# One tile for each PSUM bank, and dense products by token half from block 1 on

## The chip, the core and the metric

The kernel runs on one core of a Trainium2 chip. The core's engines run at the same time, each through its own queue in order, and meet only at semaphores: TensorE (PE, matrix products), VectorE (DVE), ScalarE (ACT), GpSimd (POOL), and SyncE (SP), whose queue here issues the DMA transfers. Matrix products land in PSUM, which this kernel uses as 8 banks of 512 float32 columns over 128 partitions. The metric is the time of one execution in microseconds on the device; less is better.

## What is computed

Attention over 4 batches and 8 heads of 576 tokens and width 64, with a threshold on the scores, and behind it two gated networks:

```python
scores = scale * q @ k.T
scores = where(scores >= max(scores) - tau, scores, -1e9)
attn   = exp(scores - max(scores)); attn /= sum(attn) + 1e-9
x  = (attn @ v) as [2304, 512]
xn = x / rms(x) * rms_g                          # first network only
y  = (silu(xn @ w_gate) * (xn @ w_val)) @ w_out  # 512 -> 1536 -> 512
z  = (silu(y @ w_gate2) * (y @ w_val2)) @ w_out2
```

All in float32. The networks' products are taken as three products of a high and a low part, so that one product of 384 columns over 128 rows stands three times in the program.

## The kernel before

The 2304 tokens go in three blocks b = 0, 1, 2 of 768, and a block is cut into two token halves of 384 columns, which is what one bank holds of a product. A network of a block is a list of 18 units: 12 for gate and value (`gate_val`), 6 for the output (`outp`), one weight matrix of 128 x 1024 each. Units 0 to 35 are block 0's two networks, 36 to 53 the first of block 1 (b = 1, m = 0), 54 to 71 its second (b = 1, m = 1), 72 to 107 block 2's. From unit 54 on most gate and value units take seven products of half size in place of eight (`gate_val7`, line 985, results read by lines 993, 995 and 1019). All other network products are line 952, in `dense`.

**Attention.** Block 0's attention stands alone at the start: 28 steps of at most two tiles of 128 queries (`fast`). A step is a product for the scores (line 581), the maximum, exponential and threshold (lines 594 to 597), transposes on PE (lines 620 and 625), copies of them out of PSUM (`EV`, lines 665 on DVE and 667 on ACT), the product with v (line 641), and one more copy into X. Block 1's attention is spread between the products of block 0's networks, and block 2's between those of block 1's first network (`tile_ops`): scores at line 685, maximum 699, exponential 701, threshold 702, sums 708, 709 and 712, scaling 521 to 525, split in two float16 parts 536 to 545, transposes by DMA 550, product with v at 734 and 736, and its copies out 746, 748 and 751.

**Banks.** The eight banks are four tiles of two: PB, PD, PA (`ps0`, `ps1`, `ps2` in the profile) and PQ (`ps3`), whose halves are called PC and PE. In block 0's attention PC takes the transposes of a step's first tile and the product with v, PE those of the second. Block 0's networks write both halves of PB and of PD in turn. In block 1's first network a product of one token half takes PB0, PB1 and PD0 in turn (`single_ps`), scores take PA and PQ in turn, and the product with v takes PD1. From unit 54 on PA and PQ are given back and taken again as four tiles of one bank (`pb0` to `pb3`) for `gate_val7`, with PB0 and PD0 as a third bank of each set; `outp` writes both halves of PB and PD again.

**Order and waits.** The code records operations with names of what they read and write, a bank each (PB0, PB1), and gives each a due time; a list scheduler with a cost for each operation then sets one order for all engines (`Program.order`), and the instructions are issued in it. The semaphore waits are not made from those names. A layer below puts them in while it issues, from what the instructions read and write of a tile.

Of the kernel before, what the change touches and what calls it, by code (L numbers as in the profile page):

```python
# [25 lines left out]
P = 128  # L26
# [14 lines left out]
KC = 510  # L41
# [34 lines left out]
for _b, _phases in enumerate(PHASES):  # L76
# [8 lines left out]
NORM_E = [(0, 0, 0, 1, 1, 0, 0, 1, 2, 1, 1, 1), (1, 1, 1, 1, 0, 2, 0, 1, 2, 1, 1, 1), (1, 0, 2, 1, 0, 0, 0, 1, 1, 0, 2, 0)]  # L85
HI_E = [(1, 2, 1, 1, 0, 0, 0, 1, 2, 0, 1, 1), (2, 1, 0, 1, 0, 1, 0, 0, 1, 2, 2, 0), (1, 0, 2, 1, 0, 1, 0, 0, 1, 0, 1, 0)]
# [3 lines left out]
V_E = {1, 3, 6, 7, 8, 12, 14, 15, 16, 21, 24, 27, 28, 29, 30, 31, 32, 34, 37, 38, 39, 40, 44, 46, 47, 48, 51, 53, 55, 56, 58, 59, 61, 68, 69, 82, 83, 87, 96, 97, 102, 107, 108, 109, 110, 113, 116, 118, 119, 120, 121, 122, 123}  # L90
K_E = {1, 3, 6, 7, 8, 12, 14, 18, 19, 20, 22, 24, 25, 26, 30, 31, 32, 33, 34}
W_E = {1, 2, 3, 6, 8, 11, 12, 13, 14, 16, 17, 18, 19, 21, 25, 27, 29, 30, 31, 33, 35, 36, 37, 38, 42, 44, 45, 46, 47, 48, 49, 51, 53, 54, 55, 56, 59, 60, 62, 64, 68, 69, 73, 74, 75, 76, 77, 83, 84, 92, 93, 95, 101, 107, 108, 110, 111, 113, 114, 117, 120, 121, 122, 125, 131, 133, 137, 138, 139, 141, 143}
H_E = {0, 1, 2, 4, 5, 8, 11, 12, 14, 15, 18, 20, 21, 23, 25, 27, 28, 31, 32, 35, 38, 39, 40, 41, 46, 48, 50, 51, 52, 54, 55, 56, 57, 58, 59, 61, 62, 63, 64, 69, 71, 73, 74, 80, 84, 85, 87, 88, 93, 94, 95}
X_E = {2, 6, 10, 11, 14, 15, 16, 18, 21, 24, 25, 29, 31, 32, 33, 34, 35, 39, 40, 41, 43, 44, 46, 48, 51, 54, 55, 57, 58, 60, 61, 62, 63, 66, 67, 74, 75, 81, 82, 83, 84, 86, 88, 89, 90, 91, 93, 94, 95}
P_E = {0, 1, 2, 3, 4, 6, 7, 8, 10, 12, 14, 15, 17, 18, 19, 21, 23, 25, 28, 29, 30}

Q_E = {7, 15, 23, 31, 39, 47, 55, 63, 66, 68, 79, 86, 95, 102, 111, 119, 120, 121, 124, 127, 128, 131, 132, 135, 138, 140, 142, 143, 147, 148, 149, 150, 151, 155, 156, 158, 159, 161, 168, 170, 173, 175, 178, 179, 181, 183, 186, 189, 190, 191}
S_E = (2, 0, 0)
# [20 lines left out]
GP = (-1.55, 1.55, 1.74, 4.96, 5.71, 5.82, 9.5, 4.12)  # L119
# [138 lines left out]
def body(ctx: ExitStack, tc: tile.TileContext, qkv, tau, w1, rg, w2, outT):  # L258
    nc = tc.nc
    sb = ctx.enter_context(tc.tile_pool(name="sb", bufs=1))  # L260
    ps = ctx.enter_context(tc.tile_pool(name="ps", bufs=1, space=bass.MemoryType.PSUM))
# [20 lines left out]
    single = []  # L282

    def bank(i):

        if not single:
            first.__exit__(None, None, None)
            ps2 = ctx.enter_context(tc.tile_pool(name="single", bufs=1, space=bass.MemoryType.PSUM))
            single.extend(ps2.tile([P, 512], F32, name=f"pb{k}") for k in range(4))
        return single[i][:, :HT]  # L290
# [977 lines left out]
```

## Time and profile before

| | us |
|---|---|
| median of 3 runs | 1200.64 (1198.11 to 1203.42) |
| the profiled execution | 1196.99 |
| its span, first to last instruction | 1195.2 |
| PE busy in the span | 1134.5 (95%) |
| DVE, ACT, POOL busy | 873.3, 715.6, 697.7 |

The profiled execution is 3.65 us, 0.3%, under the median, and 1.8 us of it lie outside the span. The time runs through four stages: block 0's attention to 150 us, block 0's networks with block 1's attention to 480, block 1's first network with block 2's attention to about 760, and the rest, products alone, to the end. A row of waits says which engine and line sat idle, and whose end released it; an idle time is worth something only on the engine that sets the stage's end.

### The profile page before, as it was taken

The page shows a single profiled execution, that of the slowest core. Times are in us where ns is not written, and L with a number is a line of the kernel's source. Part 1 is how long each engine was busy: PE and PEld are TensorE (multiplying, and loading weights), DVE is VectorE, ACT ScalarE, POOL GpSimd, SP SyncE. Part 2 cuts the span into 40 slices and gives each one's busy share as a digit, 9 for nine tenths or more (in the row PEclk, how much of TensorE's full clock was granted, in tenths as well). Part 3 has the DMA queues.
Part 4 walks back from the last instruction along what each step waited for, and adds up shares of the span by engine and source line. Part 5 has one row for each costly group of instructions (what it writes and reads, how often), then busy time and mean ns, then how long its engine had stood idle before and what let it go on. Part 6 is the DMA issues. An engine that isn't in the chain of part 4 may idle for free.

```text
span 1195.2 us, 19467 instructions
## 1 busy us (share of the span) xinstructions
PE 1134.5 (95%) x7110; PEld 1043.6 (87%) x7110; DVE 873.3 (73%) x1605; ACT 715.6 (60%) x1037; POOL 697.7 (58%) x813
## 2 busy tenths in 40 slices
PE   8778899999999999999998999999999999999998
PEld 4445699989988898988887877899999999999998
DVE  6788387888878688787767767695777557884844
ACT  4587579787888887644655455454453543544431
POOL 4366407686777787646686666144634735367750
PEclk8999999999999999999999999999999999999999
DMA  5354219999988888966676866412225132222111
GB/s 168 123 194 166 61 59 274 263 290 279 283 250 248 242 274 204 268 184 147 162 163 178 157 147 143 136 72 89 92 85 167 64 123 74 68 89 88 36 54 53
DMA packets 174433, 185.70 MB, mean 155 GB/s; under 512 B 143873, under 2 KB 147713, under 8 KB 164225
## 3 DMA queue, kind: packets, MB, share of 16 engines
q1 hardware_dynamic: 174048, 184.45, 54.3%
q8 instruction: 56, 0.92, 0.3%
q14 instruction: 41, 0.33, 0.1%
q10 hardware_dynamic: 288, 0.00, 0.0%
HBM read 120.46 MB, written 35.65 MB: 131 GB/s over the span
## 4 chain that ended last, share of the span: by engine, by line
PE 72%; DVE 10%; ACT 8%; DMA 4%; issue 3%; POOL 2%; SPq 0%; DVEq 0%; POOLq 0%; ACTq 0%
PE ps L952 38%; PE pb L985 17%; PE ps L685 3%; PE ps L734 3%; PE ps L641 3%; PE ps L985 3%; PE ps L620 2%; ACT arena L667 2%; DMA arena<-arena 1%; PE ps L736 1%; DMA arena<-in_qkv 1%; DVE arena L702 1%; DMA w<-in_w 1%; PE ps L581 1%; DVE col L699 1%
## 5 line engine op out<-in xcount | busy, mean ns | idle before, releaser
L952 PE MATMUL ps<-XS,w 128*128 128x384 f32 x1872 | 349.3, 340 | 16.6 <-DVE th L1046 4.3
L952 PEld LDWEIGHTS ps<-XS,w 128*128 128x128 f32 x1872 | 322.7, 189 | 29.5 <-DVE th L1046 6.6
L952 PE MATMUL ps<-h,w 128*128 128x384 f32 x1704 | 315.2, 338 | 3.6 <-DVE Y L1129 1.6
L952 PEld LDWEIGHTS ps<-h,w 128*128 128x128 f32 x1704 | 296.7, 188 | 9.0 <-DVE Y L1129 2.2
L985 PE MATMUL pb<-rx,arena 128*128 128x384 f32 x528 | 150.3, 339 | 1.0 <-DVE X L794 1.0
L923 POOL TENSOR_TENSOR arena<-w,arena 128x384 fp32r<-128x384 f32 (+1 forms) x84 | 110.3, 1337 | 64.0 <-ACT arena L921 63.5
L985 PEld LDWEIGHTS pb<-rx,arena 128*128 128x128 f32 x528 | 96.7, 188 | 1.2 <-issue 1.2
L702 DVE SCALAR_TENSOR_TENSOR arena<-ps,col,arena 128x576 f32<-128x576 f32 x96 | 77.6, 811 | 25.3 <-ACT arena L701 24.8
L1087 POOL TENSOR_TENSOR h<-th,h 128x768 fp32r<-128x768 f32 (+1 forms) x39 | 61.2, 1574 | 59.2 <-ACT h L1083 59.1
L701 ACT ACTIVATE arena<-ps,col 128x576 f32<-128x576 f32 x96 | 70.6, 738 | 37.5 <-DVE col L700 20.0
L1083 ACT CAST h<-th 128x768 fp32r<-128x768 f32 x72 | 60.1, 835 | 53.3 <-DVE th L1019 38.5
L699 DVE TENSOR_REDUCE col<-ps 128x1 f32<-128x576 f32 x96 | 71.4, 751 | 25.8 <-PE ps L685 25.3
L544 POOL TENSOR_TENSOR arena<-arena 128x512 f16<-128x512 f32 x68 | 86.0, 1268 | 0.2
L985 PE MATMUL pb<-XS,arena 128*128 128x384 f32 x396 | 78.9, 335 | 0.0
L685 PE MATMUL ps<-rx 128*128 128x288 f32 x416 | 71.2, 299 | 3.7 <-DVE arena L702 3.6
L685 PEld LDWEIGHTS ps<-rx 128*128 128x128 f32 x416 | 62.1, 188 | 9.1 <-DVE arena L702 5.4
L985 PEld LDWEIGHTS pb<-XS,arena 128*128 128x128 f32 x396 | 70.0, 188 | 0.0
L921 ACT CAST arena<-w 128x768 fp32r<-128x768 f32 x66 | 61.2, 941 | 14.3 <-DVE w L918 8.2
L856 ACT CAST w<-w 128x1024 fp32r<-128x1024 f32 x49 | 51.4, 1048 | 29.7 <-PE ps L952 18.7
L858 POOL TENSOR_TENSOR w<-w,w 128x1024 fp32r<-128x1024 f32 x23 | 56.6, 2462 | 20.1 <-ACT w L856 20.0
L985 PE MATMUL pb<-ra,arena 128*128 128x384 f32 x198 | 66.9, 338 | 0.0
L918 DVE TENSOR_TENSOR w<-w 128x256 f32<-128x256 f32 x80 | 53.6, 691 | 15.4 <-DMA w<-kept 14.9
(181 smaller groups left out, 2156.5 us busy)
## 6 DMA issues: line engine op xcount, KB each, us to landing
w<-in_w SPq DMA_DIRECT2D x36, 1024.0 KB, 6.3
w<-kept SPq DMA_DIRECT2D x26, 1024.0 KB, 5.4
w<-kept SPq DMA_DIRECT2D x46, 512.0 KB, 3.7
kept<-w SPq DMA_DIRECT2D x17, 1024.0 KB, 5.4
kept<-w SPq DMA_DIRECT2D x25, 512.0 KB, 3.5
arena<-in_qkv SPq DMA_DIRECT2D x40, 160.0 KB, 3.6
ra<-in_qkv SPq DMA_DIRECT2D x10, 576.0 KB, 4.4
out<-Y SPq DMA_DIRECT2D x11, 384.0 KB, 4.6
```

Of the source, the lines that this page charges most:

```text
L544: op(en, 601 if eng == 2 else 1128, lambda: n1.tensor_tensor(h[:, 640:], e[:, :512], h[:, :512], ALU.subtract), lock=True, w=[("lo", n)], ...
L685: nc.tensor.matmul(s[:, j, :HS], x[:, c:c + P], x[:, k:k + HS], start=i + u == 0, stop=i == 1 and u == len(heads) - 1)
L699: op("DVE", 670, lambda: nc.vector.tensor_reduce(c[:, 0:1], s2, AX.XY, ALU.max, negate=True), w=[*sk, ("mx", n)], bufs=[cb], p=T + F['MAX' ...
L701: op("ACT", 640, lambda: nc.scalar.activation(e2, s2, AF.Exp, bias=c[:, 2:3], scale=SCALE), r=[("thr", n)], w=[*sk, ("e", n)] + ek, bufs=[ ...
L702: op("DVE", 750, lambda: nc.vector.scalar_tensor_tensor(e2, s2, c[:, 1:2], e2, ALU.is_ge, ALU.mult, accum_out=c[:, 6:7]), r=[("thr", n)], ...
L858: op(en, 1142 if en == "DVE" else 2340, lambda: n1.tensor_tensor(ws[:, 1], w, f32(ws[:, 0]), ALU.subtract), lock=True, r=[("w32", n), ("wh ...
L921: op("ACT", 939 - 206 * late, lambda a=a, z=z: nc.scalar.copy(sbf.t()[:, 0, a:z], st[:, a:z]), r=[("w32", n)], w=[("wh", n, late)], bufs=[ ...
L923: op(en, 70 + (z - a) * 105 // 100 if en == "DVE" else 190 + (z - a) * 210 // 100, lambda a=a, z=z: n2.tensor_tensor(sbf.t()[:, 1, a:z], s ...
L952: nc.tensor.matmul(pt[:, j, :HT] if len(halves) == 2 else pt, w(i, a), x(i, b_)[:, j * HT:(j + 1) * HT], start=(i == 0 and a == 0 and b_ = ...
L985: nc.tensor.matmul(bank(), w()[:, a, col * 256 + i * P:][:, :P], xf(i, b_), start=first and i == 0 and a == 0 and b_ == 0, stop=i == 1 and ...
L1083: op("ACT", 734, lambda: nc.scalar.copy(h[:, 0], tb.t), r=[("th", n)], w=[("h0", n)], bufs=[tb, hb], p=p + O(n)['HH'], name=f"h{n}")
L1087: op(eng, 72 + (z - a) * 105 // 100 if eng == "DVE" else 190 + (z - a) * 209 // 100, lambda a=a, z=z: n1.tensor_tensor(h[:, 1, a:z], tb.t[ ...
```

## The change

Every bank that is used alone becomes a tile of its own, and the tiles change between stages. At the start PC and PE are two tiles (`pt0`, `pt1`); PA, PB, PD are pairs (`ps0`, `ps1`, `ps2`). Before block 1's networks (`phase` 1) PD becomes PD0 and PD1 (`pbPD0`, `pbPD1`); products of one half take PC, PE and PD0 in turn, scores PA and PB, the product with v PD1. Before unit 54 (`phase` 2) PA and PB become four tiles. Dense products go by token half in all of blocks 1 and 2, so also in the plain units and in `outp` after unit 54, whose results are read 384 columns at a time. The sums of block 2's attention (lines 708 and 709) move from DVE to POOL (`S_E`), and tables and due times are other numbers, of which two lines stand here.

```diff
-S_E = (2, 0, 0)
+S_E = (0, 0, 0)
-UP, UP1, FP, T0, ATT, ATT2, LEAD, LEAD2, END2, UL, RMS0, RMS1, RMS2, CREL = 10544, 14740, 1362, 179133, 22274, -4036, 8, 7.0, 4.0, 13618, -50718, -149645, -594509, 80130
+UP, UP1, FP, T0, ATT, ATT2, LEAD, LEAD2, END2, UL, RMS0, RMS1, RMS2, CREL = 10544, 9643, 1362, 179133, 22274, -69668, 8, 7.5, 8.0, 15712, -50718, -149645, -320154, 80130
...
-    PB, PD = [ps.tile([P, 2, 512], F32, name=f"ps{i}") for i in range(2)]
-    PA = ps1.tile([P, 2, 512], F32, name="ps2")
-    PQ = ps1.tile([P, 2, 512], F32, name="ps3")
-    PC, PE = PQ[:, 0], PQ[:, 1]
+    PC, PE = [open_["C"].tile([P, 512], F32, name=f"pt{i}") for i in range(2)]
+    PA, PB, PD = [open_[k].tile([P, 2, 512], F32, name=f"ps{i}") for i, k in enumerate("ABD")]
+    def bank(key):
+        if key not in ones_:
+            keys = ["PD0", "PD1"] if key in ("PD0", "PD1") else ["PA0", "PA1", "PB0", "PB1"]
+            for k in "D" if key in keys[:2] and len(keys) == 2 else "BA":
+                pools[k].__exit__(None, None, None)
...
+            for k in keys:
+                ones_[k] = p.tile([P, 512], F32, name=f"pb{k}")
+        return ones_[key]
...
-    THREE = [(PB[:, 0, :HT], "PB0"), (PB[:, 1, :HT], "PB1"), (PD[:, 0, :HT], "PD0")]
...
-    def single_ps():
-        third[0] += 1
-        return THREE[third[0] % 3]
+    def single_ps(late_=True):
+        third[0] += 1
+        if phase[0] == 1:
+            key = ("PC", "PE", "PD0")[third[0] % 3]
+        else:
+            key = (("PB0", "PB1") if late_ else ("PC", "PE")) + ("PD0", "PD1")
+            key = key[third[0] % 4]
+        return (lambda: bank(key)[:, :HT]), key
...
-        s, sk = (PQ, ["PC", "PE"]) if n >= 2 * NTB and n % 2 else (PA, BK["PA"])
+        s, sk = (PB, BK["PB"]) if n >= 2 * NTB and n % 2 else (PA, BK["PA"])
...
-        pv_, vk = (PD[:, 1], "PD1") if b == 2 else ((PC, "PC"), (PE, "PE"))[pvt[0]]
+        vk = "PD1" if phase[0] else ("PC", "PE")[pvt[0]]
...
+    SETS = [[(lambda k=k: bank(k)[:, :HT], k) for k in x] for x in (("PC", "PE", "PD0"), ("PA0", "PA1", "PB0"))]
...
-                if b == 1 and m == 0:
+                if b:
...
-                    if b == 1 and m == 0:
+                    if b:
```

Up to about 484 us of the trace every engine has the same instructions in the same order in both programs, which was found by comparing the two orders with line and tile names set aside; what differs there is the tiles and the waits. The first place is DVE in block 0's attention, where L665 (L679 in the change) copies transposes or a step's result out of a bank; a name in brackets is the counter of the engine waited for. Before:

```order
L665 COPY X_83<-ps3_71 128x128 [waits Activation_49]
L594 TENSOR_REDUCE col_106<-ps0_65 128x1 [waits PE_49]
L594 TENSOR_REDUCE col_106<-ps2_70 128x1 [waits PE_49]
L597 SCALAR_TENSOR_TENSOR arena_87,col_106<-ps0_65,col_106,arena_87 128x576 [waits Activation_49,Pool_49]
L597 SCALAR_TENSOR_TENSOR Y_85,col_106<-ps1_66,col_106,Y_85 128x576 [waits PE_49,Activation_49]
L665 COPY X_83<-ps3_71 128x128 [waits Activation_49]
```

The change:

```order
L679 COPY X_90<-pt0_74 128x128 [waits PE_49]
L608 TENSOR_REDUCE col_113<-ps1_77 128x1 [waits PE_49]
L608 TENSOR_REDUCE col_113<-ps0_76 128x1 [waits PE_49]
L611 SCALAR_TENSOR_TENSOR arena_94,col_113<-ps1_77,col_113,arena_94 128x576 [waits Activation_49,Pool_49]
L611 SCALAR_TENSOR_TENSOR Y_92,col_113<-ps2_78,col_113,Y_92 128x576 [waits PE_49,Activation_49]
L679 COPY X_90<-pt0_74 128x128 [waits PE_49]
```

Both copies out of PC into X waited for a copy of ACT, which reads the other bank of `ps3`; now they wait for PE alone.

The second place is PE in block 1's first network, a gate and value unit: L952 (L967) is the dense product, `ps0` is PB, `ps1` is PD, whose other bank takes the product with v. Before, the rows that stand at 640 us of the trace:

```order
L952 MATMUL ps0_65<-XS_84,w2_105 128x384 [waits DVE_49]
L952 MATMUL ps0_65<-XS_84,w2_105 128x384 x5
L952 MATMUL ps1_66<-XS_84,w2_105 128x384 [waits Activation_49]
L952 MATMUL ps1_66<-XS_84,w2_105 128x384 x5
L952 MATMUL ps1_66<-XS_84,w2_105 128x384 [waits Activation_49]
L952 MATMUL ps1_66<-XS_84,w2_105 128x384 x5
L952 MATMUL ps0_65<-XS_84,w2_105 128x384 [waits DVE_49]
L952 MATMUL ps0_65<-XS_84,w2_105 128x384 x11
```

The change, a unit of the same kind:

```order
L967 MATMUL pt0_74<-XS_91,w2_112 128x384 x6
L967 MATMUL pt1_75<-XS_91,w2_112 128x384 x6
L699 MATMUL ps1_77<-rx2_1229 128x288 [waits DVE_49]
L699 MATMUL ps1_77<-rx2_1229 128x288 x3
L967 MATMUL pt1_75<-XS_91,w2_112 128x384 x6
L967 MATMUL pbPD0_4993<-XS_91,w2_112 128x384 x12
L967 MATMUL pt0_74<-XS_91,w2_112 128x384 [waits DVE_49]
L967 MATMUL pt0_74<-XS_91,w2_112 128x384 x11
```

Before, all four runs of products begin with a wait, for a reader of the bank beside; now three tiles turn, and the wait that is left on a dense product stands where a bank comes round again.

The third place is PE in `outp` of block 1's second network, one output of 128 rows and 24 products. Before:

```order
L952 MATMUL ps1_66<-h0_91,w2_105 128x384 [waits DMAHW0_49,Activation_49]
L952 MATMUL ps1_66<-h0_91,w2_105 128x384 x5
L952 MATMUL ps1_66<-h1_92,w2_105 128x384 x6
L952 MATMUL ps1_66<-h2_93,w2_105 128x384 x6
L952 MATMUL ps1_66<-h3_94,w2_105 128x384 x6
L952 MATMUL ps0_65<-h0_91,w2_105 128x384 [waits Activation_49]
L952 MATMUL ps0_65<-h0_91,w2_105 128x384 x5
```

The change:

```order
L967 MATMUL pbPB1_7371<-h0_98,w2_112 128x384 [waits DMAHW0_49,Activation_49]
L967 MATMUL pbPB1_7371<-h0_98,w2_112 128x384 x2
L967 MATMUL pbPB1_7371<-h1_99,w2_112 128x384 x3
L967 MATMUL pbPB1_7371<-h2_100,w2_112 128x384 x3
L967 MATMUL pbPB1_7371<-h3_101,w2_112 128x384 x3
L967 MATMUL pbPD0_4993<-h0_98,w2_112 128x384 [waits Activation_49]
L967 MATMUL pbPD0_4993<-h0_98,w2_112 128x384 x2
L967 MATMUL pbPD0_4993<-h1_99,w2_112 128x384 x3
L967 MATMUL pbPD0_4993<-h2_100,w2_112 128x384 x3
L967 MATMUL pbPD0_4993<-h3_101,w2_112 128x384 x3
```

The same products no longer alternate between the halves of a pair: one half goes through all four h tiles into one bank, then the other half into the next.

## Rows read from the trace of the kernel before

**Rows 1.** busy time by stage; the first row names the columns

```profile
core 0: us, PE busy (x) PEld busy (x) DVE busy (x) ACT busy (x) POOL busy (x), PEclk, DMA share, GB/s
0.00:150.00 150.00, 119.10 (x1072) 79.42 (x1072) 101.14 (x228) 96.49 (x177) 76.33 (x170) 0.95 0.44 142
150.00:480.00 330.00, 324.64 (x1928) 303.43 (x1927) 268.84 (x448) 277.45 (x337) 225.38 (x262) 0.99 0.86 243
480.00:800.00 320.00, 299.04 (x1879) 269.55 (x1878) 246.73 (x596) 170.77 (x276) 193.62 (x211) 1.00 0.66 161
800.00:1150.00 350.00, 350.00 (x2001) 349.83 (x2000) 235.30 (x305) 159.56 (x231) 192.83 (x163) 1.00 0.26 89
```

**Rows 2.** waits of PE, 480 to 800 us: total us, times, longest

```profile
PE ps L952 <- DVE th L1046: 4.3, 7, 0.8
PE ps L952 <- DVE th L1049: 3.2, 3, 1.7
PE ps L952 <- ACT th L1048: 3.0, 4, 0.9
PE ps L952 <- ACT X L748: 2.7, 5, 1.0
PE ps L952 <- DVE Y L1129: 1.6, 2, 1.0
PE ps L952 <- ACT tq L746: 1.5, 3, 0.8
PE ps L952 <- ACT Y L1127: 1.1, 1, 1.1
```

**Rows 3.** timeline of PE, 636 to 646 us, idle before and releaser in brackets

```profile
640.11 1.31 PE L952 MATMUL ps<-XS,w 128*128 128x384 f32 x6 [1.74 <-DVE th L1049]
642.26 1.31 PE L952 MATMUL ps<-XS,w 128*128 128x384 f32 x6 [0.84 <-ACT tq L746]
```

**Rows 4.** waits of PE, 0 to 150 us

```profile
PE ps L620 <- ACT arena L667: 4.9, 10, 1.2
```

**Rows 5.** waits of DVE, 0 to 150 us

```profile
DVE X L665 <- ACT arena L667: 3.9, 5, 1.3
DVE arena L665 <- ACT arena L667: 2.7, 5, 0.9
```

**Rows 6.** timeline, 91 to 95 us: one step of the first attention

```profile
91.28 0.66 PE L620 MATMUL ps<-ident,Y 128*128 128x128 f32 x4
...
91.97 0.27 ACT L667 COPY X<-ps 128x128 f32<-128x128 f32 x1
92.13 0.59 ACT L667 COPY arena<-ps 128x512 f32<-128x512 f32 x1
...
92.78 0.66 PE L620 MATMUL ps<-ident,arena 128*128 128x128 f32 x4 [0.84 <-ACT arena L667]
...
93.65 0.69 DVE L665 COPY arena<-ps 128x512 f32<-128x512 f32 x1 [0.89 <-PE ps L625]
...
94.69 0.33 PE L641 MATMUL ps<-arena 128*64 128x128 f32 x2 [0.46 <-ACT arena L667]
```

**Rows 7.** busy time in a 20 us stretch of block 0's attention

```profile
70.00:90.00 20.00, 15.52 (x155) 9.71 (x155) 17.82 (x41) 18.63 (x29) 13.86 (x22) 1.00 0.66 214
```

**Rows 8.** groups of POOL, whole span: busy us, mean ns, idle before

```profile
L708 POOL TENSOR_SCALAR col<-col 128x1 f32<-128x1 f32 x48 | 18.2, 379 | 44.4 <-DVE arena L702 41.0
...
L709 POOL TENSOR_SCALAR col<-col 128x1 f32<-128x1 f32 x48 | 16.2, 338 | 3.7
```

**Rows 9.** timeline of DVE, 630 to 640 us

```profile
634.67 4.13 DVE L544 TENSOR_TENSOR arena<-arena 128x512 f16<-128x512 f32 x1
```

**Rows 10.** groups of DVE, 480 to 800 us, shapes apart: busy us, mean ns, idle before

```profile
L544 DVE TENSOR_TENSOR arena<-arena 128x512 f16<-128x512 f32 x16 | 14.3, 896 | 0.0
...
L1129 DVE SCALAR_TENSOR_TENSOR Y<-ps,Y 128x384 f32<-128x384 f32 x16 | 8.8, 553 | 10.2 <-PE ps L952 5.3 <-PE ps L736 4.7
...
L1144 DVE SCALAR_TENSOR_TENSOR Y<-ps,Y 128x768 f32<-128x768 f32 x4 | 3.8, 952 | 1.2 <-PE ps L952 1.2
```

More of the change, by code (lines that the diff above doesn't have):

```diff
@@ L273, in ring, with use @@
         return Ring([sb.tile(shape, dt, name=f"{name}{i}") for i in range(n)])
-    PB, PD = [ps.tile([P, 2, 512], F32, name=f"ps{i}") for i in range(2)]
-    first = tc.tile_pool(name="first", bufs=1, space=bass.MemoryType.PSUM)
-    ps1 = first.__enter__()
-    PA = ps1.tile([P, 2, 512], F32, name="ps2")
-    PQ = ps1.tile([P, 2, 512], F32, name="ps3")
-    PC, PE = PQ[:, 0], PQ[:, 1]
[L282 to L290, printed above, removed]
+    PC, PE = [open_["C"].tile([P, 512], F32, name=f"pt{i}") for i in range(2)]
+    PA, PB, PD = [open_[k].tile([P, 2, 512], F32, name=f"ps{i}") for i, k in enumerate("ABD")]
+    ones_ = {"PC": PC, "PE": PE}
+    def bank(key):
[3 more added lines that the diff above has]
+                pools[k].__exit__(None, None, None)
+            side = "right" if len(keys) == 2 else "left"
+            p = ctx.enter_context(tc.tile_pool(name=f"q{key}", bufs=1, space=PSUM, side=side))
+            for k in keys:
+                ones_[k] = p.tile([P, 512], F32, name=f"pb{k}")
+        return ones_[key]
     BK = {k: [k + "0", k + "1"] for k in ("PA", "PB", "PD")}
-    THREE = [(PB[:, 0, :HT], "PB0"), (PB[:, 1, :HT], "PB1"), (PD[:, 0, :HT], "PD0")]
     turn = [0]
     third = [0]
-    def single_ps():
-        third[0] += 1
-        return THREE[third[0] % 3]
+    phase = [0]
+    fresh = {1: ["PD0", "PD1"], 2: ["PA0", "PA1", "PB0", "PB1"]}
+    def use(key):
+        for k in (1, 2):
+            if k in fresh and phase[0] >= k and key in fresh[k]:
+                return fresh.pop(k)
+        return [key]
+    def single_ps(late_=True):
+        third[0] += 1
+        if phase[0] == 1:
[4 more added lines that the diff above has]
+        return (lambda: bank(key)[:, :HT]), key
     pvt = [0]
@@ L757, in rms @@
         T = ST(b * NTB + NTB - 1) + (RMS0 - 60000, RMS1, RMS2)[b]
-        p = PE[:, 384:396]
+        pk = "PD1" if phase[0] else "PE"
+        p = lambda: bank(pk)[:, 384:396]
         def sums():
             for t in range(6):
-                nc.tensor.matmul(p[:, 2 * t:2 * t + 2], SS[:, t * P:(t + 1) * P], ones, start=True, stop=True)
-        op("PE", 1280, sums, r=SK(0, TW), w=["PE"], p=T, name=f"rms_sum{b}", cols=0)
+                nc.tensor.matmul(p()[:, 2 * t:2 * t + 2], SS[:, t * P:(t + 1) * P], ones, start=True, stop=True)
+        op("PE", 1280, sums, r=SK(0, TW), w=[pk], p=T, name=f"rms_sum{b}", cols=0)
         mb, yb, qb = [r_tok.next() for _ in range(3)]
@@ L960, in moe @@
         for m in range(2):
+            if b == 1 and m == 1:
+                phase[0] = 2
             hh = {}
@@ L1120, in outp @@
                             Tj, Uj = T + j * U / 2, U / 2
-                            dense(x, [key], 4,
+                            dense(x, use(key), 4,
                                   lambda i, a, o=o, w=w: w[:, a, i * 256 + (o % 2) * P:i * 256 + (o % 2 + 1) * P],
@@ L1126, in outp @@
                             if q == 0:
-                                op("ACT", 390, lambda y=y, x=x: nc.scalar.copy(y, x), w=[key, ("Y", o)] + [("eb", 2 * i) for i in range(4)], p=Tj + Uj + O(n)['DR'] + O(n)['YY'], name=f"y{n}")
+                                op("ACT", 390, lambda y=y, x=x: nc.scalar.copy(y, x()), w=[key, ("Y", o)] + [("eb", 2 * i) for i in range(4)], p=Tj + Uj + O(n)['DR'] + O(n)['YY'], name=f"y{n}")
                             else:
-                                op("DVE", 480, lambda y=y, x=x: nc.vector.scalar_tensor_tensor(y, x, 1.0, y, ALU.mult, ALU.add), w=[key, ("Y", o)], p=Tj + Uj + O(n)['DR'] + O(n)['YY'], name=f"y{n}")
+                                op("DVE", 480, lambda y=y, x=x, last=-1.0 if m == 1 and q == 2 else 1.0: nc.vector.scalar_tensor_tensor(y, x(), last, y, ALU.mult, ALU.add if last > 0 else ALU.subtract), w=[key, ("Y", o)], p=Tj + Uj + O(n)['DR'] + O(n)['YY'], name=f"y{n}")
                         if q == 2:
-                            put(o, Y[:, o], [("Y", o)], [], T + U + O(n)['DR'] + O(n)['PUT'], ("POOL", "DVE")[8 * b + 4 + o in P_E])
+                            if m == 0:
+                                put(o, Y[:, o], [("Y", o)], [], T + U + O(n)['DR'] + O(n)['PUT'], ("POOL", "DVE")[8 * b + 4 + o in P_E])
+                            else:
+                                op("DMA", 1200, lambda o=o: nc.sync.dma_start(outT[o, :, b * TW:(b + 1) * TW], Y[:, o]), r=[("Y", o)], p=T + U, name="out")
                         continue
@@ L1213, in body @@
         if 0 < b < NB - 1:
-            op("ACT", 200, lambda: nc.scalar.copy(PQ[:, 1, KC:KC + 2], K0), w=["PE"], p=ST((b + 1) * NTB), name="K1")
+            phase[0] = 1
+            op("ACT", 200, lambda: nc.scalar.copy(PB[:, 1, KC:KC + 2], K0), w=["PB0", "PB1"], p=ST((b + 1) * NTB), name="K1")
             tiles((b + 2) * NTB)
```

64 lines of the change are left out of this document (32 added, 32 removed), and 6 rows, old and new, of the table OFFS.

## Prediction

> **What bounds the kernel now.** I read the busy time by stage first [rows 1], because the shares over the whole span hide it. In every stage TensorE (PE) is the fullest engine: it is busy 119.1 of 150 us in block 0's attention, 324.6 of 330 while block 0's networks run, 299.0 of 320 from 480 to 800 us, and all 350 of the 350 behind that. The clock was granted at 0.95 to 1.00 of full speed in all four, so it explains nothing here. The two programs hold the same 7268 PE instructions, so PE's busy time stays, and what the change can give is idle time of PE: 30.9 us in the first stage, 5.4 in the second, 21.0 in the third, none in the fourth up to 1150 us. The third stage has the most to give for the least work, and there I read PE's waits second [rows 2]. Seven rows hold 17.4 us in 25 waits, all of dense products, and they are short (the longest 1.7 us). What they name is the clue: evacuations of dense products (L1046, L1048, L1049, L1127, L1129) and copies of the product with v (L746, L748), which live in the other half of PD and have nothing to do with a dense product.
>
> Third comes the timeline of one such place [rows 3], beside the order printed above. At 640.11 a product into one half of PB starts after 1.74 us of waiting for L1049; at 642.26 a product into PD0 starts after 0.84 us of waiting for L746, which reads PD1. Going through all these waits with the bank that each product writes and the bank that the named instruction reads, I found the two to be different banks of one tile, and the last reader of the product's own bank had ended before the wait began. So the names by bank, which the program's list of operations carries, do not reach the semaphores: a wait belongs to a tile, and a pair of banks is one. These waits go with the pairs.
>
> **Block 1's first network, 480 to 800 us.** Of 21.0 us idle, 17.4 are such waits [rows 1, 2]. If all went and nothing followed, the gain would be 17.4, and with the rest (data that comes late) 21.0: that is the far end. The near end is nothing: behind each wait may stand a wait of the same length for something else. I take a value from the stage beside, where block 0's networks run with another attention woven in and PE idles 5.4 us in 330, 1.6% [rows 1]; 1.6% of 320 is 5.2 us. To this I add 1.3 us for what the next paragraph says of POOL, so the idle time goes from 21.0 to 6.5 us, and the term is **-14.5 us** (bounds 0 and -21). What speaks for the near stage rather than for zero is the order: a bank of a dense product now comes round after two others in three separate tiles, so that a reader has two products of six instructions, about 2 x 1.31 us by the pace in [rows 3], and a reading takes 0.55 [rows 10]. The scores lose nothing, as they still have two pairs of banks in turn (PA and PB for PA and PQ).
>
> **Sums of block 2's attention go to POOL.** That is 96 instructions, 48 tiles with one L708 and one L709 each. Block 1's sums run on POOL already, at 379 and 338 ns [rows 8], so POOL gains 48 x 0.717 = 34.4 us, and DVE is rid of them. POOL was busy 193.6 of 320 us [rows 1]; it would come to 228. On average that leaves 92 us, but the attention's work bunches between 550 and 700 us, and there POOL will be near its limit. Queued behind the sums on POOL are the scaling, the splits of the exponentials and the adds (L749) of the product with v, and PE waits for those in the end. This costs between 0 (the sums hide in the 92 us) and the whole 14.5 us that the waits give back; 1.3 is near the first end, since the average is far from full.
>
> A row that speaks against this move is the DVE subtraction L544 at 634.67 us, which took 4.13 us [rows 9], where 16 of its kind average 0.90 [rows 10]. Something held it up while it ran. The Trainium skill, page "SBUF — State Buffer", section "Who interferes with whom", says that a DVE instruction with two inputs in SBUF and a GpSimd instruction share one pair of ports, that whoever starts first holds it, and that the other then stands still. The row agrees with a block of that kind and does not prove it; if every added POOL instruction held DVE for its length, that would be 34.4 us on DVE, which was busy 246.7 of 320, so that DVE would come to 281 and the sum would stay as it is. What it does to the chance of trouble is the second rival.
>
> **Block 0's attention, 0 to 150 us.** The order is word for word the same, only the waits differ. PC and PE, the transposes' banks, were one tile. PE's transposes waited 4.9 us in 10 waits for ACT's copies L667 [rows 4], DVE's copies 6.6 us for ACT's [rows 5], two readers that never touch the same bank. One step shows it whole [rows 6]: transposes into PE's next bank wait 0.84 us for a copy that reads the other, DVE's copy waits 0.89 behind the next transposes, and the product with v starts at 94.69. Without the waits across banks I put that start at 93.6 to 93.9, so 0.8 to 1.1 us of a step. Were it the same for all 28 steps, the stage would shrink by 22 us, the far end, well inside the 30.9 us that PE idles. But a stage of this kind does not give all that: from 70 to 90 us ACT is busy 18.6 of 20 and DVE 17.8 [rows 7], so that the evacuating engines are late themselves; ACT's spare 7% of the 120 us that this goes on is 8 us. The near end is 0, if ACT sets the pace already. I take **-8 us**. The start of block 0's networks then moves ahead by that much. Their weights must come earlier too; the stage behind hardly waits for anything (5.4 us idle), but its DMA share is 0.86 [rows 1], so I let 8 us pass, and doubt that twice as much would.
>
> **Block 0's networks, 150 to 480 us.** PB and PD stay pairs, both halves of a pair belong to one product, and the order is the same. Zero.
>
> **Behind unit 54, 800 us to the end.** PE is never idle up to 1150 [rows 1], so nothing can be gained there. The dense products by half are read 384 columns at a time: 553 ns twice in place of one of 952 [rows 10], 0.15 us more for a pair, for 23 pairs 3.5 us of DVE, which is busy 235 of 350. That is hidden. What is not certain is the distance from a reading to the next product in that bank: at 21 places more than before only one half product stands between. Each could cost half a microsecond of waiting, 21 x 0.5 = 10 us at worst, and 0 at best; before had 16 such places and no idle time, so I take **+0.5**.
>
> **The sum.** 1196.99 (the profiled execution, span 1195.2 and 1.8 around it) - 8 - 14.5 + 0.5 = 1175.0. The profiled execution was 3.65 us under the median of the runs shown, so I add this back: **1178.6**.
>
> **The rivals.** *The start gives twice as much.* If ACT, freed of its own waits behind transposes, is no bound and a step does shrink by some 0.6 us, 28 steps give 16: about 1170.6. For it speak the step in [rows 6] and the 30.9 us of idle PE, against it ACT's 93% [rows 7].
>
> *POOL and DVE take back most of block 1's gain.* If POOL's queue runs full between 550 and 700 us, the attention's chains end later and PE waits for them in place of banks; with 16 of the 21 us still idle the third stage gives 5: 1196.99 - 8 - 5 + 0.5 + 3.65 = 1188.1. For it speak 34.4 us more on POOL and [rows 9]; against it that DVE is relieved on the same chain, and that a tile's way from its scores to its use is long.
>
> *The change doesn't do what it says.* Behind the waits for banks stand the data's, or the tiles taken anew bring waits of their own (the old pool must be empty first). Then the time stays between 1195 and 1200. Against it stands the order, where the waits on a dense product in place two are fewer and later.
>
> *Slower.* POOL becomes the bound of block 1's first network. It needs 228 us of 320 at the durations of [rows 8] and those before; it decides as soon as its instructions there last over 320/228 = 1.4 times as long on average. At 1.5 times they need 342 us: +22 on this stage in place of -14.5, and with -8 and +0.5 it ends at 1196.99 + 14.5 + 3.65 = 1215.1. One DVE instruction at 4.6 times its mean [rows 9] shows that such stretching exists, 16 instructions averaging 0.90 that it is rare.
>
> **How the numbers follow.** What a measurement of this kernel can tell from no change is about 0.5%, 6 us, so faster means under 1194.6. The forecast, between 1173 and 1185, has 0.62; the larger start 0.13; POOL and DVE taking most of block 1 0.13; no effect 0.07; slower 0.05. The first three are faster, 0.88. The range should leave out no more than 0.2: the low end lets the start give 16 and block 1 17.4 less a little (1167.5); the high end lets the start give 4 and block 1 6 (1191), which takes in the second rival. The last two cases and some of the edges lie outside.
>
> **What would show it.** In the changed kernel's waits of PE from 480 us on, the rows of a dense product waiting for L746 or L748 should be gone altogether, and those for L1046, L1048 and L1049 down to a few in number; PE's idle time in that stage should be near 6.5 us. In block 0's attention the waits of DVE's copies for ACT's copies should be gone, and the first dense product of block 0 should start about 8 us earlier. Behind 800 us PE should still be full. I am wrong in the first step if PE still waits for readers of other banks, in the second if POOL's queue is full and PE's waits name the attention's adds and transposes, in the third if ACT's share in 70 to 90 us stays at 93% and the networks start when they did, or if they start over 12 us earlier.

## The result, and the profile after

The change takes 1151.66 us (1149.51 to 1152.39) where the kernel before took 1201.05 in the same comparison: a ratio of 0.9587, with a 95% interval of 0.9562 to 0.9612. That is 49.4 us less. I had forecast 1178.6, so 22 us less, and a range that ended at 1167.5. The direction and the mechanism were right, the size was less than half of what came.

To see where the time went I cut both traces at the same products of the networks: the first, the 1601st (near the end of block 0's second network, where the two orders part) and the 2701st (unit 56, behind the last of the attention). Before (the columns are those of [rows 1]):

```profile
0.00:133.80 133.80, 104.72 (x935) 67.07 (x935) 99.18 (x222) 90.52 (x160) 71.09 (x166) 0.95 0.46 150
133.80:494.60 360.80, 353.39 (x2150) 328.75 (x2149) 282.30 (x475) 295.36 (x368) 239.29 (x281) 0.99 0.84 236
494.60:791.60 297.00, 276.27 (x1745) 248.17 (x1744) 227.74 (x565) 154.13 (x255) 182.87 (x196) 1.00 0.65 159
791.60:1195.20 403.60, 400.14 (x2287) 399.64 (x2285) 264.06 (x345) 175.62 (x255) 204.42 (x173) 1.00 0.24 83
```

The changed kernel, cut at the same places:

```profile
0.00:113.80 113.80, 102.79 (x935) 66.57 (x935) 97.54 (x218) 88.94 (x160) 70.87 (x163) 1.00 0.55 176
113.80:473.10 359.30, 352.22 (x2149) 327.98 (x2148) 288.07 (x481) 296.05 (x371) 239.25 (x282) 1.00 0.84 237
473.10:744.30 271.20, 267.44 (x1745) 249.25 (x1744) 232.83 (x476) 155.80 (x254) 200.97 (x283) 1.00 0.70 174
744.30:1147.70 403.40, 400.14 (x2287) 399.74 (x2286) 271.12 (x371) 177.40 (x269) 202.60 (x174) 1.00 0.24 83
```

The start lost 20.0 us, block 0's networks 1.5, the third stage (block 1's first network with block 2's attention) 25.8, the rest 0.2. The 1.5 can't be told from nothing: in the twelve traces of the table below that stage takes 357.8 to 361.6 us, whatever the tiles. What to see is PE's column in the third row: the same 1745 products, a stage 25.8 us shorter, and only 17.0 of that is idle time (20.7 before, 3.8 after). The other 8.8 us is *busy* time, 276.27 against 267.44 for the same products. I had written that PE's busy time stays. (The profile models the ends of PE's products, so where idle time stops and busy time begins is the profile's; the 25.8 us are not.)

The waits of PE in that stage, which were the seven rows of [rows 2] and more, are these in the change, in full:

```profile
PE pt L967 <- DVE th L1065: 2.4, 2, 1.2
PE ps L801 <- DVE small L793: 1.2, 1, 1.2
```

Waits for L746 and L748 are gone, as the order had led me to expect. In the first stage the waits of DVE's copies for ACT's copies [rows 5] are gone too. The longest waits of DVE that are left there:

```profile
DVE col L608 <- PE ps L595: 7.9, 7, 4.6
DVE col L620 <- POOL col L616: 1.5, 2, 0.8
DVE X L679 <- PE pt L655: 0.8, 2, 0.4
```

and a step of the attention (timeline, start and length in us, then the operation, in brackets the idle time ahead and who ended it), to lay beside [rows 6]:

```profile
78.52 0.66 PE L634 MATMUL pt<-ident,Y 128*128 128x128 f32 x4
...
79.05 0.37 ACT L681 COPY X<-pt 128x128 f32<-128x128 f32 x1
...
79.22 0.70 ACT L681 COPY arena<-pt 128x512 f32<-128x512 f32 x1
...
79.48 0.66 PE L634 MATMUL pt<-ident,arena 128*128 128x128 f32 x4 [0.30 <-ACT X L681]
...
80.17 0.69 DVE L679 COPY arena<-pt 128x512 f32<-128x512 f32 x1 [0.16 <-PE pt L634]
...
80.92 1.35 PE L655 MATMUL pt<-arena 128*64 128x128 f32 x18
```

The second transposes now wait for the copy that reads their own bank (X), 0.30 us, and no longer for the wide copy out of the other one. From the first transposes to the product with v it takes 2.40 us, where [rows 6] show 3.41.

### The profile page after: what moved, and what is told of

Read it like the earlier page. It is cut to its first block, busy times and chain, and to the rows that moved or that the text cites. A ratio compares the mean times of both kernels' runs of the same rounds, so it can differ in the third digit from the quotient of the medians.

```text
span 1147.7 us, 19538 instructions
## 1 busy us (share of the span) xinstructions
PE 1122.6 (98%) x7110; PEld 1043.5 (91%) x7110; DVE 889.6 (78%) x1543; ACT 718.2 (63%) x1052; POOL 713.7 (62%) x900
## 4 chain that ended last, share of the span: by engine, by line
PE 79%; DVE 7%; ACT 5%; DMA 4%; issue 2%; POOL 1%; SPq 0%; POOLq 0%; ACTq 0%; DVEq 0%
PE ps L967 15%; PE pbPD L967 12%; PE pt L1002 10%; PE pt L967 10%; PE pbPA L1002 8%; PE pbPB L967 6%; PE ps L699 4%; PE pbPD L749 2%; PE pt L655 2%; PE pt L749 2%; PE pbPD L1002 2%; PE ps L595 1%; PE pt L634 1%; PE pbPB L1002 1%; DMA arena<-arena 1%
## 5 line engine op out<-in xcount | busy, mean ns | idle before, releaser
L967 PE MATMUL ps<-XS,w 128*128 128x384 f32 x1152 | 212.0, 339 | 0.9 <-DVE th L1081 0.9
L967 PEld LDWEIGHTS ps<-XS,w 128*128 128x128 f32 x1152 | 199.1, 189 | 5.3 <-issue 2.6
L967 PE MATMUL ps<-h,w 128*128 128x384 f32 x576 | 106.0, 338 | 0.5 <-DVE th L1092 0.4
L967 PEld LDWEIGHTS ps<-h,w 128*128 128x128 f32 x576 | 99.9, 188 | 2.3 <-DVE th L1092 0.7
L967 PE MATMUL pbPD<-h,w 128*128 128x384 f32 x528 | 99.8, 337 | 0.0
L967 PEld LDWEIGHTS pbPD<-h,w 128*128 128x128 f32 x528 | 92.6, 187 | 0.6 <-issue 0.5
L967 PE MATMUL pt<-XS,w 128*128 128x384 f32 x468 | 88.7, 337 | 2.4 <-DVE th L1065 2.4
L1103 POOL TENSOR_TENSOR h<-th,h 128x384 fp32r<-128x384 f32 (+1 forms) x39 | 63.4, 1628 | 37.4 <-ACT h L1099 37.1
L1002 PE MATMUL pt<-rx,arena 128*128 128x384 f32 x288 | 85.4, 338 | 0.0
L967 PEld LDWEIGHTS pt<-XS,w 128*128 128x128 f32 x468 | 80.7, 188 | 3.5 <-DVE th L1065 3.1
L967 PE MATMUL pbPB<-h,w 128*128 128x384 f32 x420 | 80.2, 336 | 0.0
L967 PEld LDWEIGHTS pbPB<-h,w 128*128 128x128 f32 x420 | 74.0, 188 | 0.0
```

The source lines that it names most:

```text
L967: nc.tensor.matmul(pt[:, j, :HT] if len(halves) == 2 else pt(), w(i, a), x(i, b_)[:, j * HT:(j + 1) * HT], start=(i == 0 and a == 0 and b_ ...
L1002: nc.tensor.matmul(bank(), w()[:, a, col * 256 + i * P:][:, :P], xf(i, b_), start=first and i == 0 and a == 0 and b_ == 0, stop=i == 1 and ...
L1103: op(eng, 72 + (z - a) * 105 // 100 if eng == "DVE" else 190 + (z - a) * 209 // 100, lambda a=a, z=z: n1.tensor_tensor(h[:, 1, a:z], tb.t[ ...
```

## The experiments

Lengths of the four stages from each trace, cut at those products, in us. Idle is the length of the third stage less PE's busy time in it. Stops are the places where more than 0.03 us lie between two products of PE, counted in the trace.

| kernel | start | block 0's networks | third stage | idle, stops there | rest | median |
|---|---|---|---|---|---|---|
| before | 133.8 | 360.8 | 297.0 | 20.7, 33 | 403.7 | 1201.05 |
| the change | 113.8 | 359.4 | 271.2 | 3.8, 4 | 403.4 | 1151.66 |
| e1_start | 112.7 | 361.0 | 300.1 | 21.4, 34 | 403.6 | 1179.53 |
| e2_startpair | 135.4 | 357.8 | 271.4 | 3.9, 5 | 403.5 | 1169.59 |
| e3_b1pair | 113.3 | 360.3 | 297.5 | 21.2, 38 | 423.8 | 1197.34 |
| e9_b1single | 134.2 | 360.9 | 273.4 | 4.7, 8 | 419.9 | 1190.51 |
| e5_tiles | 112.4 | 360.4 | 294.6 | 18.2, 15 | 408.7 | 1180.70 |
| e6_numbers | 135.8 | 358.0 | 292.0 | 16.7, 31 | 404.3 | 1193.12 |
| e4_sums | 113.0 | 361.2 | 288.4 | 14.1, 16 | 403.2 | 1168.45 |
| e10_tilesums | 113.9 | 360.5 | 288.4 | 13.5, 17 | 408.7 | 1175.20 |
| e11_sumsfix | 116.4 | 361.6 | 273.3 | 5.1, 7 | 403.4 | 1153.42 |
| e12_beforesums | 135.1 | 360.7 | 309.6 | 30.6, 27 | 403.4 | 1212.35 |

### The start: tiles alone, order untouched

e1_start gives the kernel before two tiles for PC and PE until block 1 begins.

```diff
-    PQ = ps1.tile([P, 2, 512], F32, name="ps3")
-    PC, PE = PQ[:, 0], PQ[:, 1]
...
+    PC, PE = [ps3.tile([P, 512], F32, name=f"pt{i}") for i in range(2)]
...
```

> The kernel before with one edit: the banks PC and PE are two tiles from the start until block 1's networks, then a pair again. Every engine's order is that of the kernel before. Theory (the waits across the two banks are the whole gain of the first stage): the first dense product starts at about 114 us in place of 133.8 and the time falls by 20, to about 1181 (ratio 0.983). Rival (part of it is the clock, which was granted at half for 10 us in the profile of before and not in that of after, or something else in the change): it falls by 8 to 12, to 1189 to 1193.

e2_startpair undoes the same in the change.

```diff
-    PC, PE = [open_["C"].tile([P, 512], F32, name=f"pt{i}") for i in range(2)]
+    PQ = open_["C"].tile([P, 2, 512], F32, name="pt")
+    PC, PE = PQ[:, 0], PQ[:, 1]
...
```

> The changed kernel with one edit undone: PC and PE are one tile again until block 1's networks begin, single tiles from there. Every engine's order is that of the changed kernel. Theory: the whole 20 us come back, about 1171.5 (0.9755 of before), with the same waits of the evacuations for one another as in before, and nothing changes behind. Rival (the first stage's gain is partly hidden later, as the next stage's loads can't follow): less than 15 come back, 1160 to 1166.

Measured: 0.9824 of before (0.9798 to 0.9849), 1179.53, for the first, and 0.9747 (0.9727 to 0.9766), 1169.59, for the second, 18 us over the change. The first stage's row in both, e1 then e2:

```profile
0.00:112.70 112.70, 101.41 (x934) 66.11 (x934) 97.61 (x218) 88.50 (x160) 70.78 (x163) 0.97 0.54 178
```

```profile
0.00:135.40 135.40, 105.70 (x935) 67.84 (x935) 98.10 (x220) 90.14 (x160) 70.14 (x163) 0.95 0.45 148
```

The two waits of [rows 5] stand again in e2's waits of DVE, to the same sums but one tenth:

```profile
DVE X L681 <- ACT arena L683: 3.9, 5, 1.3
...
DVE arena L681 <- ACT arena L683: 2.6, 5, 0.9
```

So the split of one tile is worth 20 us with no instruction moved, and nearly all of it reaches the end. All traces of the table agree, and up to there every engine's order is the same in all of them: five with the pair have a start of 133.8 to 135.8 us, seven with two tiles one of 112.4 to 116.4. So a difference of less than 4 us in the start can't be read from one trace. The clock has no share that shows: e1's granted clock of 0.97 lies near the 0.95 of before, and its start is as short as that of the change with 1.00.

### The start: does ACT set the pace?

My step had capped this gain at 8 us by ACT's spare time. e7_actload burdens ACT with a copy that nobody reads, behind each wide copy of transposes:

```diff
-            op("ACT", 70 + n * 83 // 100, lambda: nc.scalar.copy(o, x), w=w, bufs=bufs, p=p, name=name)
+            def both():
+                nc.scalar.copy(o, x)
+                if kind == "EV" and n == 512:
+                    nc.scalar.copy(junk, ident)
+
+            op("ACT", 70 + n * 83 // 100, both, w=w, bufs=bufs, p=p, name=name)
...
```

> The changed kernel with one more copy on ACT, 128 by 128 from one place in SBUF to another that nobody reads, behind each of the 33 or so wide copies of transposes that ACT makes in block 0's attention; nothing waits for it but ACT's own queue. It adds 7 to 9 us of work on ACT. My prediction took ACT to set the pace of the whole stage; if it does, the first dense product comes 7 to 9 us later. Theory now (ACT is full from 60 to 80 us only, and elsewhere the wait from step to step sets the pace): 2 to 4 us later, 1153.5 to 1156.

Measured: 1153.39 us, 1.7 over the change, and a first dense product at 115.8, 2.0 later, at the lower edge of what I expected. The added group, from its profile (busy us, mean ns):

```profile
L685 ACT COPY junk<-ident 128x128 f32<-128x128 f32 x32 | 10.5, 327 | 0.0
```

The 32 records add up to 10.5 us, but they overlap those beside them: ACT's next instruction starts 0.20 us behind the start of an added copy, so that ACT got 6.4 us more to do. The start came 2.0 us later, which lies within the spread of starts of this order (112.4 to 116.4) and can't be told from none. If ACT set the pace of the whole stage, it would have been 6.4; it does not. ACT is full in one stretch: cut in 20 us pieces, the change has ACT full from 60 to 80 us and PE, not ACT, near full ahead of it:

```profile
20.00:40.00 20.00, 18.81 (x188) 12.64 (x186) 17.56 (x42) 13.35 (x27) 11.76 (x30) 1.00 0.45 151
40.00:60.00 20.00, 19.21 (x193) 12.61 (x190) 18.51 (x44) 16.80 (x28) 11.11 (x28) 1.00 0.55 179
60.00:80.00 20.00, 16.68 (x173) 10.74 (x171) 18.54 (x40) 19.78 (x32) 15.61 (x24) 1.00 0.78 253
```

In the stretch of before that I had read, 70 to 90 us [rows 7], my cap was right: the same products of PE there stand 12.05 us earlier in the change at 73.2 and 12.73 at 90.6 of before, a gain of 0.7 us in 17.4. Up to 73 us the gain was 12, behind 91 it was 7.

### The start: a try to relieve it

e8_late moves the first weights' conversions out of that full stretch.

```diff
-CR0, CR1 = 50145, 10950
+CR0, CR1 = 60145, 9950
```

> The changed kernel with the first three weights' conversions (some 4 us of ACT and 1 of DVE each) released at 60, 70 and 80 us of the schedule in place of 50, 61 and 72, the order made anew. From 60 to 80 us ACT is busy 19.8 of 20 us and PE 16.7, from 80 to 114 ACT has room. Theory: the start gets 1 to 3 us shorter, 1149 to 1151. Rival (the first weights then come late for block 0's networks, or the new order is worse by chance): 1152 to 1158.

Measured: 1176.78 us, 25 over the change. The theory fell, and the rival had the direction but not the size, 19 us above its range: the first stage came out 4.5 us longer (118.2), block 0's networks 8 (367.3), the next stage 17.5 (288.7). The number changes the order up to the end of the attention, and which part of that costs what was not taken apart.

### Block 1's first network: tiles and order apart

e3_b1pair keeps the change's order on every engine and makes PC with PE and PD0 with PD1 pairs again from block 1 on; the start stays split.

```diff
+            for k in ("PC", "PD") if key in RIGHT else []:
+                t = p.tile([P, 2, 512], F32, name=f"pp{k}")
+                ones_[k if k == "PC" else "PD0"], ones_["PE" if k == "PC" else "PD1"] = t[:, 0], t[:, 1]
...
```

> The changed kernel with one edit undone from block 1's first network to the end: PC with PE and PD0 with PD1 are pairs again, the start keeps single tiles. Every engine's order is that of the changed kernel. Theory (the tiles make block 1's gain): waits across banks come back, the time rises by 20 to 35, to 1172 to 1187; PE's idle time from 480 to 750 us rises by 12 to 25 us, and the length of the stage by 0.27 us more for each place at which PE stops (0.16 for the last product that nothing overlaps, 0.10 for the first after the stop). Rival (the new order and numbers make it): under 6 us, at most 1158.

e9_b1single keeps the order of the kernel before and makes PB and PD single tiles in this stage.

```diff
-    THREE = [(PB[:, 0, :HT], "PB0"), (PB[:, 1, :HT], "PB1"), (PD[:, 0, :HT], "PD0")]
+    THREE = [(lambda k=k, i=i: gen(k, 1)[i][:, :HT], k + str(i)) for k, i in (("PB", 0), ("PB", 1), ("PD", 0))]
...
```

> The kernel before, order and numbers untouched on every engine, with PB and PD as four single tiles in block 1's first network alone. It has pairs again from unit 54 on, PA and PQ among them, which before split there, so only the stretch from the end of block 0's networks to unit 54 (494.6 to 791.6 us of before, 297.0 us long, 33 stops of PE) counts. Theory (the waits across banks can simply be taken out): 16 us of idle time and some 25 stops go, the stretch takes 272 to 280 us. Rival (in the old order the next wait, for the attention's chain, stands close behind): 287 to 295 us.

Measured: e3 0.9979 of before (0.9968 to 0.9990), all but 2.5 us of the gain gone; e9 0.9919 (0.9894 to 0.9943). The stage's row of e3, with the row behind it, and that of e9:

```profile
473.60:771.10 297.50, 276.30 (x1745) 248.89 (x1745) 228.39 (x476) 155.58 (x254) 200.44 (x283) 1.00 0.62 159
771.10:1194.80 423.70, 408.39 (x2287) 397.61 (x2285) 266.39 (x371) 177.27 (x269) 202.72 (x174) 1.00 0.22 79
```

```profile
495.10:768.50 273.40, 268.73 (x1745) 248.81 (x1743) 227.46 (x565) 154.24 (x256) 182.44 (x196) 1.00 0.71 173
```

This is the clearest pair of the study. With pairs the stage takes 297.0 in the old order and 297.5 in the new one; with single tiles 273.4 in the old and 271.2 in the new. The tiles give 23.6 to 26.3 us, the new order and all its numbers 2.2 at most, and only once the tiles are there. The rival, that other waits stand close behind, fell: of 33 stops in the old order 8 are left. The price of a stop named ahead of e3, 0.27 us beside its idle time, came out at 0.26. In total e3's expectation was missed by 10 us, for a place that it didn't count: its pairs cost 20 us more behind unit 54, where products in PC and PE, and in PD0 and PD1, wait for one another's readers; e9 has a cost of the same kind there (16 us, from PA and PQ as pairs), and its total is to be read with that.

### The numbers and the sums

e5_tiles takes the code of the change with the old tables (the lines from `NORM_E` to `GP`), e6_numbers the old code with the new tables. One line of e5's edit, which e6 has the other way round:

```diff
...
-UP, UP1, FP, T0, ATT, ATT2, LEAD, LEAD2, END2, UL, RMS0, RMS1, RMS2, CREL = 10544, 9643, 1362, 179133, 22274, -69668, 8, 7.5, 8.0, 15712, -50718, -149645, -320154, 80130
+UP, UP1, FP, T0, ATT, ATT2, LEAD, LEAD2, END2, UL, RMS0, RMS1, RMS2, CREL = 10544, 14740, 1362, 179133, 22274, -4036, 8, 7.0, 4.0, 13618, -50718, -149645, -594509, 80130
...
```

> The code of the change (single tiles, halves in turn) with the tables, due times and engine choices of the kernel before, the order made by the scheduler from these. Theory (the waits across banks are the gain, the numbers only a refinement): 20 us at the start and most of block 1's 26, 1158 to 1168. Rival (the numbers carry block 1's gain, as the old ones were fitted to pairs): at 1175 or above, and PE's idle time in block 1's first network stays near 20 us, now behind data.

> The kernel before, pairs and all, with the tables, due times and engine choices of the change. Theory: no gain at the start, where orders are the same, and none in block 1, since waits across banks stay: 1195 to 1215. Rival (the numbers carry block 1's gain): 1172 to 1180.

e4_sums is the change with the sums back on DVE; e10_tilesums is e5, and e12_beforesums the kernel before, each with the reverse of this line. In these three the scheduler makes a new order.

```diff
-S_E = (0, 0, 0)
+S_E = (2, 0, 0)
```

e11_sumsfix leaves the change's order as it is and issues only the sums on DVE:

```diff
-        ns = nc.gpsimd if se == 0 else nc.vector
+        ns = nc.gpsimd if n < 2 * NTB else nc.vector
```

> The changed kernel with the sums of block 2's attention (48 tiles) back on DVE, the order made anew by the scheduler from the other numbers of the change. My forecast had the move cost up to a few us, since POOL was to run full. If that is so: 1.3 us less, 1150. Rival (DVE, at 43 to 45 of 50 us between 550 and 700, is the engine that needs relief): the added 14 us on DVE bring stops of PE, 3 to 12 us more, 1155 to 1164.

> The code of the change with the numbers of the kernel before, as in e5_tiles (1180.7), but with the sums of block 2's attention on POOL. In e5_tiles and e4_sums, both with the sums on DVE, a last part of the attention stood uncovered behind the products of the network. Theory (the sums on DVE make this tail): it goes, 1158 to 1166. Rival (the tail comes from the old due times): 1175 to 1185.

> The changed kernel with its order on every engine kept, and only the 96 sums of block 2's attention issued on DVE, at their place in the order. It tells what the move costs or gives on the chip apart from what the scheduler makes of it. Theory (DVE's time is what the move saves; it would be busy some 47 of 50 us): 3 to 10 us more than the change, 1155 to 1162. Rival (the 17 us of e4_sums came from the order alone): within 2 us of the change, or faster, as a sum is 0.14 us on DVE and 0.36 on POOL.

> The kernel before, with its pairs and numbers, and only the sums of block 2's attention moved to POOL, the order made anew. Theory (waits across banks set the stage, so the sums' engine matters little there): 1194 to 1203. Rival (the sums on DVE held the attention up in before too): 1180 to 1190.

Measured against before: e5 0.9841 (0.9810 to 0.9873), e6 0.9959 (0.9936 to 0.9981), e4 0.9735 (0.9712 to 0.9758), e10 0.9795 (0.9765 to 0.9826), e11 0.9604 (0.9574 to 0.9634), e12 1.0105 (1.0076 to 1.0135).

Three things follow. First, the move of the sums itself is worth little: with the order pinned, e11 is 1.8 us behind the change, which the two intervals (that of the change is 0.9562 to 0.9612) can't tell from none, and its third stage 2.1 longer. The theory of 3 to 10 us fell. Second, the 17 us of e4 came from the order that the scheduler made for it, since e11 has the same sums on DVE without them. In e4 and e5 57 products of the attention more than in the change (27 in e10) are left for the end of the stage, with little to lie beside them, and PE stands in that last stretch, for which the change takes 20.5 us. e4, then e5:

```profile
718.80:762.60 43.80, 33.38 (x178) 28.64 (x178) 35.72 (x62) 17.30 (x27) 18.24 (x13) 0.88 0.36 103
```

```profile
724.80:767.40 42.60, 32.58 (x180) 27.99 (x179) 34.69 (x65) 20.14 (x31) 15.05 (x11) 0.88 0.32 97
```

A part of it is the clock: 0.88 granted in both rows, so the lower of its two levels (1.2 GHz) for about 10 of the 43 us, in a stretch in which PE stood for a quarter of the time, where the change has 1.00 throughout. That is worth 5 us at most.

Third, old numbers on the new tiles (e5) keep the start's gain and lose nearly all of the other, 294.6 against 297.0, although the tiles alone give 23.6 in the old order (e9). The new numbers on the old tiles (e6) give 5 us there. So the gain can be had without the numbers (e9). That on the change's tiles they keep the scheduler from spoiling it is what e5 suggests, not more, as e5 also uses the banks otherwise than e9. Several expectations missed by this: e5's and e10's theories (the time of e5's rival came, but its reason, that the numbers carry the gain, falls with e9), e6's, which came out 2 us below its range, e12's, which came out 9 us above its range with 46.0 us in the last stretch, and both of e4's: it forecast a gain of 1.3 us, and its rival had a loss, 4 us too small, and laid it to DVE's load. In e11 DVE carries the same sums and PE hardly waits. Which of the numbers makes a good order was not taken apart.

## Why the prediction was wrong

**The mechanism was right.** The waits belonged to tiles, the order's rows showed which would go, and they went: e1 and e9 take them out without moving one instruction. The stage behind unit 54 gave nothing and cost nothing (403.7 and 403.4), where I had 0.5; block 0's networks gave nothing that can be told from none, as I had it. Two terms were mis-sized.

**The start, -8 forecast, -20.0 measured.** The step that failed is the cap: "ACT's spare 7% of the 120 us that this goes on is 8 us". The 93% came from 20 us [rows 7] and was laid over 120. Over the whole stage [rows 1] have ACT at 96.5 of 150 us, 64%, and that row was as near at hand; in e7 6.4 us more on ACT made the start 2.0 longer, which can't be told from none. The sign that I had named for this step being wrong, networks that start over 12 us earlier, came. The step before it, 0.8 to 1.1 us saved on each of 28 steps, gave the far end of 22, and the truth is 20.0, or 0.7 a step. The rival with twice the gain named this way and had 0.13.

**Block 1, -14.5 forecast, -25.8 measured.** The idle time was sized fairly: 6.5 us left forecast, 3.8 found. What the sum had no term for is what a stop costs beyond its idle time, because "PE's busy time stays". It did not: 29 stops fewer, 8.8 us less busy, 0.30 us each. e9 has 25 fewer and 7.5 less (0.30), e3 34 more than the change and 8.9 more (0.26). [rows 3] had shown it: six products between two stops take 1.31 us. In the change twelve run without one and the next operation starts 2.09 us behind them, so six take 1.05 (timeline of PE):

```profile
601.65 2.24 PE L967 MATMUL pt<-XS,w 128*128 128x384 f32 x12
603.74 1.40 PE L749 MATMUL pbPD<-arena 128*128 128x320 f16 x9
```

The difference, 0.26, is the end of the last product, which lies beside the start of the next when there is one, and a slower start of the first (in the median 281 ns pass from its start to the next in the third stage of before, and 174 otherwise). The Trainium skill, page "TensorE: Matmul & The Clock Gate", section "Step-by-step: what each phase is for", says that a matmul's drain overlaps the fill of the next, so that a lone one pays for it. The trace agrees as far as modelled ends go: products of L967 last 337 to 340 ns on average, and 174 ns pass from start to start. With 25 waits of [rows 2] at 0.26 us the sum would have had 6.5 us more in this term.

**The sums.** I added 1.3 us for them; by e11 the move cost nothing and gave 2 at most. DVE was rid of 3.0 us by it (last section). POOL's work for them was 25.7 us and not the 34.4 worked out from [rows 8], since each was shorter in this stage:

```profile
L722 POOL TENSOR_SCALAR col<-col 128x1 f32<-128x1 f32 x48 | 13.1, 273 | 6.8 <-DVE arena L716 3.1 <-DVE col L726 0.2
L723 POOL TENSOR_SCALAR col<-col 128x1 f32<-128x1 f32 x48 | 12.6, 262 | 3.8
```

**The rivals.** POOL and DVE taking back the gain did not come: POOL was busy 201 of 271 us and PE idle 3.8. The slower one needed POOL's instructions to stretch to 1.4 times; they did not, and the 4.13 us that spoke for it were DVE standing behind POOL (last section). That nothing comes of it because other waits stand behind is refuted by e9. A sum with the far end of the start (22), the idle time as forecast (14.5) and 6.5 for the stops would have been 43 us, where 47.5 was measured between the two profiled runs.

## What to carry to other kernels

Look whether two buffers that different engines use at different times are one tile: the waits are placed by tile, and one order with two layouts of tiles differed here by 20 us in one stage and 24 to 26 in another, with no instruction moved. When PE's waits are counted, add for each stop what it costs beside its idle time, which shows as busy time (0.26 to 0.30 us here). A cap on a gain is read from the whole stretch to which it is applied, not from its fullest part; and when a planner makes a new order after an edit, the edit is measured with the old order pinned, or the planner's luck (15 us between e4 and e11, which differ in the order alone) is taken for the edit's. The length of a record is not what the instruction adds: where records overlap, take the busy time with and without them.

## What the runs showed of the hardware

**Records overlap.** The 96 sums make 13.7 us of records on DVE in e11 (48 of 144 and 48 of 141 ns), and yet DVE's busy time in the stage fell only from 235.5 to 232.8 when they went to POOL. Nothing took the rest back: each record starts before the one ahead of it ends (timeline of DVE in e11):

```profile
521.94 0.15 DVE L722 TENSOR_SCALAR col<-col 128x1 f32<-128x1 f32 x1
522.01 0.14 DVE L723 TENSOR_SCALAR col<-col 128x1 f32<-128x1 f32 x1
522.12 0.16 DVE L726 RECIPROCAL col<-col 128x1 f32<-128x1 f32 x1
```

Without the sums DVE's records fill 232.5 us of e11's stage, as they fill 232.8 in the change. So the sums added 3.0 us to DVE's busy time and not 13.7.

**DVE stood behind POOL.** Some of DVE's instructions became longer with the sums on POOL, others shorter. This one, from SBUF to SBUF, became longer (groups of DVE in the stage, busy us and mean ns; the change, then e11):

```profile
L515 DVE TENSOR_TENSOR rx<-ra,rx 128x576 fp32r<-128x576 f32 x9 | 11.3, 1254 | 0.0
```

```profile
L515 DVE TENSOR_TENSOR rx<-ra,rx 128x576 fp32r<-128x576 f32 x9 | 8.8, 981 | 0.2 <-ACT tq L761 0.2
```

Its length goes by what POOL was doing when it began. Two cases from the timeline of the change:

```profile
549.64 0.74 DVE L515 TENSOR_TENSOR rx<-ra,rx 128x576 fp32r<-128x576 f32 x1
...
616.98 1.85 POOL L1103 TENSOR_TENSOR h<-th,h 128x768 fp32r<-128x768 f32 x1
617.12 2.32 DVE L515 TENSOR_TENSOR rx<-ra,rx 128x576 fp32r<-128x576 f32 x1
```

At 549.64 POOL was idle, and L515 took 0.74 us. At 617.12 POOL was 0.14 us into L1103, and L515 ended 0.61 us behind that one's end. Seven of the nine in the change began while POOL was at work, and all seven ended 0.60 to 0.61 us behind the end of the POOL instruction; the two others took 0.73 and 0.74. In e11 it was five of nine. The one of the seven that began during a sum took 0.75, so it was wide POOL instructions, met at other moments, that made the mean longer, and not the length of the sums. The 4.13 us of [rows 9] are of this kind as well: in the trace of before POOL ran three instructions without a pause from 634.41 to 638.26 us, and L544 ended at 638.80.

That agrees with the rule of the Trainium skill that the prediction cites (page "SBUF — State Buffer", section "Who interferes with whom"), of a pair of ports that both engines share. The times of e11 and the change show no cost of it to the kernel.
